# Gated mix of linear attention and FFN on one core: keys and values by seven block products, FFN weights streamed through the first sweep, the query fold moved to TensorE

## The chip, the cores and the metric

The kernel runs on one core of a Trainium2 chip. The core has TensorE (PE in the profile; its weight loads are shown apart as PEld), VectorE (DVE), ScalarE (ACT), GpSimd (POOL) and SyncE (SP, which here only issues DMAs). The metric is the device time of one execution in microseconds. The kernel before took 514.8 us, the median of three runs (514.75 to 515.55).

## The reference

The input is one sequence of 2048 rows with 512 features. A gate mixes two branches: linear attention with 32 heads of 16 features, and an FFN with 1792 hidden units.

```python
g = sigmoid((x * gate_w).sum(-1, keepdims=True))
out = g * A(x) + (1 - g) * B(x)

def A(x):                     # linear attention with a learned feature map
    q, k, v = heads(x @ wqkv)                          # 32 heads of 16
    pq, pk = q @ w_phi, k @ w_phi                      # one 16x16 matrix per head
    phi_q = concat([softmax(pq), softmax(-pq)])
    phi_k = concat([softmax(pk), softmax(-pk)])
    kv, z = phi_k.T @ v, phi_k.sum(over rows)          # per head
    return ((phi_q @ kv) / (phi_q @ z + 1e-6)) @ wo

def B(x):
    h = relu(x @ w1 + b1)
    return (h * h) @ w2 + b2
```

Keys must be summed over all 2048 rows before the first query row can be finished.

## The kernel before

**Arithmetic.** Every large product is computed in three matmuls: an operand is split into a high part, rounded by an ACT copy, and a low part, the difference, formed on DVE (`split`, one ACT and one DVE instruction). `mm3` then issues high x high, high x low and low x high into one PSUM bank. Each of these matmuls has 128 stationary columns and 512 moving columns.

**Loops.** The rows go in four blocks of 512 (`NB`), each of four chunks of 128 (`NC`). The FFN's hidden units go in 14 slices of 128. There are two sweeps over the four blocks: the first with hidden slices 0 to 6, the second with 7 to 13. A sweep, block and slice make one *work step* t, 56 in all. In work step t TensorE runs up(t+2), the first FFN product, 12 matmuls into a bank of `ps_u` (two banks), and down(t), the second product, 12 matmuls into the four banks of `ps_d`. Between them ACT and DVE make the hidden values of up(t) (`hidden`: ReLU, square, high part on ACT, then the low part `hl` on DVE). At the end of a block DVE evacuates the four `ps_d` banks (L714), and the first sweep's results go to DRAM as `part`. The FFN weights of a sweep's seven slices (`w1`, `w2`, high and low) are all held in SBUF, in a pool of seven.

**Slots.** Each work step has two slots, 2t before up(t+2) and 2t+1 before down(t). A table (`at(slot, function, ...)`) places all other work in these slots. The code is written in slot order, and a list scheduler turns it into one in-order queue for each engine, by priorities: `high_priority` raises one, and `issue_after` ties an instruction behind another.

**First sweep.** For each chunk, `do_k` projects the keys (12 matmuls, `k`) into the bank of `ps_a`; DVE reads them four times and ACT and DVE make the two softmaxes (`exps`, `scaled`). `do_v` projects the values (12 matmuls, `v`), which ACT copies to `vext`. For every two chunks `do_kv` adds phi_k.T @ [v, 1] into one bank, `kvps`, which stays in `ps_b` during the whole sweep. The gate's dot products, block loads and splits, and the saving of the split x to DRAM (`xkept`) lie between.

**The folds.** w_phi is multiplied into wk and wq once. For wk this is 64 small matmuls (`foldk`, in the place of up(3) at work step 1) into four PSUM banks, and four DVE transposes. For wq it is done on DVE: 64 DMAs that read rows of wq with repetition, and 64 multiply-adds (L234, L236) spread over slots 13 to 46, then transposes and a trip through DRAM.

**Second sweep.** For each chunk `do_q` projects the queries, `q_phi` makes features and denominators (POOL multiplies by z, L363), the features are transposed by DVE and DMAs, and `numer` and `attended` finish the attention.

Of the kernel before, what the change touches and what calls it, by code (L numbers as in the profile page):

```python
# [16 lines left out]
P = 128  # L17
# [7 lines left out]
LAG = 2  # L25
NG = 8
VW = DH + 1
NV = 3
AHEAD = 150


@with_exitstack
def tile_gated_mix(ctx: ExitStack, tc: tile.TileContext, xT, xn, wqT, wkT, wphi, wv, wo, w1, b1, w2, b2, gw, out):
# [6 lines left out]
    fpool = pool("fpool", NFH)  # L40
# [27 lines left out]
    def mm3(o, a, b, sa, sb, first, last):  # L68
        (ah, al), (bh, bl) = a, b
        nc.tensor.matmul(o, ah[:, sa], bh[:, sb], start=first, stop=False)  # L70
        nc.tensor.matmul(o, ah[:, sa], bl[:, sb], start=False, stop=False)  # L71
        return nc.tensor.matmul(o, al[:, sa], bh[:, sb], start=False, stop=last)  # L72
# [12 lines left out]

    def ffn_tiles(nm, fc):
        return (fpool.tile([P, 512], F32R, tag=nm + "h", name=f"{nm}h{fc}"),
                fpool.tile([P, 512], F32R, tag=nm + "l", name=f"{nm}l{fc}"))
# [13 lines left out]
    def ready(nm, fc):  # L102
        hi, lo = ffn_tiles(nm, fc)
        i = split(raw.pop((nm, fc)), hi, lo, nc.scalar, nc.vector)
        (up_w if nm == "w1" else down_w)[fc] = hi, lo
        return i

    def ready_later(nm, fc):
        with tc.issue_after(st["act"].ins):
            ready(nm, fc)  # L110
# [20 lines left out]
    def x_fetch(b):  # L131
        for k in range(NK):
            if k % 2 == 0:
                t = work.tile([P, 2 * D], F32, tag="tb", name="xin", bufs=2)
            raw["x", b, k] = t[:, (k % 2) * D:(k % 2 + 1) * D]
            nc.sync.dma_start(raw["x", b, k], xT[b, :, k, :])
# [20 lines left out]
    wqm = dram.tile([NK * 4, 32, D], F32, name="wqm")  # L157
    zrow = dram.tile([2 * D], F32, name="zrow")
    xkept = dram.tile([NB, NK, 2, P, SB], F32, name="xkept")
    vext = [hold.tile([P, H * VW], F32, tag="vz", name=f"vext{i}") for i in range(NV)]  # L160
# [7 lines left out]
    def load_fold(wT):  # L168
        t = [row() for _ in range(1 + NK)]
        nc.sync.dma_start(t[0], wphi)  # L170
        for g in range(NK):
            nc.sync.dma_start(t[g + 1], wT[:, g, :])
        return t

    def foldk():
        wph, *t = st["wT"]  # L180
        pss = [ps_u.tile([P, 512], F32, tag="u", name=f"foldk{r}") for r in range(2)]
        pss += [p.tile([P, 512], F32, tag="s", name="foldk") for p in banks]
# [14 lines left out]
        w = work.tile([P, 2, 4, NG, 32], F32, tag="phiT", name="wkin", bufs=1).rearrange(  # L197
# [5 lines left out]
        banks.pop()  # L203
        st["wk"] = [w[:, k].rearrange("p g r s -> p (g r s)") for k in range(NK)]

    def foldk_ready(k):
        hi = wpool.tile([P, 512], F32R, tag=f"wah{k}", name=f"wkh{k}")
        lo = wpool.tile([P, 512], F32R, tag=f"wal{k}", name=f"wkl{k}")
        with tc.high_priority(offset=AHEAD):
            split(st["wk"][k], hi, lo, nc.scalar, nc.vector)  # L210
        st.setdefault("wa", []).append((hi, lo))

    def foldq_numbers():
        wph = st["wT"][0]
        t = stage.tile([P, 512], F32, tag="in", name="wpht")
        st["phc"] = small.tile([P, NK, DH], F32, tag="dz", name="phc", bufs=2)  # L220
        with tc.issue_after(st["low"].ins):
            nc.vector.transpose(t, wph)

            nc.vector.tensor_reduce(st["phc"], t.rearrange("p (g j e) -> p g e j", g=NK, e=DH), AX.X, ALU.add)

    def foldq_step(i):
        g, e = divmod(i, DH)
        t = stage.tile([P, 512], F32, tag="in", name="wqr")
        nc.sync.dma_start(t, wqT.rearrange("(j e) g d -> g e j d", e=DH)[g, e].unsqueeze(1).to_broadcast([8, DH, D]))
        s = st["phc"][:, g, e:e + 1]  # L230
        with tc.issue_after(st["low"].ins):
            if e == 0:
                st["acc"] = row()
                nc.vector.tensor_scalar(st["acc"], t, s, None, ALU.mult)  # L234
            else:
                nc.vector.scalar_tensor_tensor(st["acc"], t, s, st["acc"], op0=ALU.mult, op1=ALU.add)  # L236
        if e == DH - 1:
            if g == 0:
                st["wqt"] = work.tile([P, 2, 4, NG, 32], F32, tag="phiT", name="wqt", bufs=1).rearrange(
                    "p u r g s -> p (u r g s)").rearrange("p (c g j) -> p c g j", c=4 * NK, g=NK)  # L240
            nc.vector.transpose(st["wqt"][:, :, g, :], st["acc"].rearrange("p (c j) -> p c j", c=4 * NK))

    def foldq_move():
        for r in range(4):
            nc.sync.dma_start(wqm.rearrange("c i (r n) -> r i c n", r=4)[r],
                              st["wqt"][32 * r:32 * r + 32].rearrange("p c g j -> p c (g j)"))
        st["wq"] = [row() for _ in range(NK)]
        for k in range(NK):
            nc.sync.dma_start(st["wq"][k], wqm[4 * k:4 * k + 4].rearrange("c i n -> (c i) n"))

    def foldq_ready(k):
        hi = wpool.tile([P, 512], F32R, tag=f"wah{k}", name=f"wqh{k}")
        lo = wpool.tile([P, 512], F32R, tag=f"wal{k}", name=f"wql{k}")
        v = lambda t: t.rearrange("p (g r j) -> p g r j", g=NK, r=4)
        with tc.high_priority(offset=AHEAD):
            split(st["wq"][k].rearrange("p (r g j) -> p g r j", g=NK, r=4), v(hi), v(lo), nc.scalar, nc.vector)
        st.setdefault("waq", []).append((hi, lo))
        if k == NK - 1:
            st["wa"] = st["waq"]
# [8 lines left out]
    def v_ready(k):  # L268
        hi, lo = w_tiles("v", k)
        with tc.issue_after(st["act"].ins):  # L270
            split(raw.pop(("v", k)), hi, lo, nc.scalar, nc.vector)
        st.setdefault("wb", []).append((hi, lo))

    def w_tiles(nm, k):
        return (wpool.tile([P, 512], F32R, tag=f"wbh{k}", name=f"w{nm}h{k}"),
                wpool.tile([P, 512], F32R, tag=f"wbl{k}", name=f"w{nm}l{k}"))

    def load_w(src, nm):
        res = []
        for k in range(NK):  # L280
            if nm == "o":

                t = stage.tile([P, 512], F32, tag="in", name="in")
                for q in range(4):
                    s = 64 * (4 * (k % 2) + q) + 32 * (k // 2)
                    nc.sync.dma_start(t[32 * q:32 * q + 32, :], src[s:s + 32, :])
            else:
                t = load(src[k * P:(k + 1) * P, :])
            hi, lo = w_tiles(nm, k)
# [5 lines left out]
    def gate_load(n):  # L295
        t = st["xn", n] = work.tile([P, D], F32, tag="ol" if n % 2 else "oh", name="xn", bufs=2)
        nc.sync.dma_start(t, xn[n])
# [52 lines left out]
    def kv_chunk(n, kvps, phi, v):  # L350
        for i in range(NG):
            for j in range(4):
# [3 lines left out]
                                 start=(n == 0 and i == 0), stop=(n == NB * NC - 1),  # L356
# [105 lines left out]
    def do_w(src, nm):  # L462
# [304 lines left out]
```

## Time and profile before

| what | value |
|---|---|
| median of three runs | 514.8 us |
| profiled execution: first to last instruction (span) | 513.7 us |
| around the span, median less span | 1.1 us |
| granted TensorE clock | 1.000 |
| PE, PEld, DVE, ACT, POOL busy | 509.4, 411.3, 401.0, 227.3, 44.1 us |
| POOL, first sweep | idle but for memsets |
| DMA moved | 75.4 MB, 147 GB/s over the span |

The profile is one execution. A row of its time line reads: start, duration, engine, source line, operation, output <- inputs, shapes, count, and in brackets the idle time before it with what ended it. A row of its groups reads: line, engine, operation, output <- inputs, shapes, count | busy time, mean ns of one | idle before. Matmuls overlap: each takes about 0.39 us from start to end, while the next begins before that, so their pace is read from the starts of their weight loads. DVE and ACT instructions overlap a little in the same way.

### The profile page before, as it was taken

What the parts mean: (1) busy time and instruction counts of PE and PEld (TensorE: products, weight loads), DVE (VectorE), ACT (ScalarE), POOL (GpSimd) and SP (SyncE); (2) the same over time, 40 slices, a digit from 0 to 9 for tenths busy, and PEclk for the clock granted to TensorE, in tenths of its full rate; (3) what the DMA queues carried; (4) which work ended last, traced back from release to release, by engine and by line L of the source; (5) the groups of instructions that cost most, each with busy time, mean ns of one, the idle gap of its engine ahead of it and who ended that gap; (6) DMA issues with size and microseconds to landing.
All of it is one profiled execution on the core that took longest, in us unless ns stands there. A gap on an engine that the chain in (4) does not pass through costs nothing.

```text
span 513.7 us, 9257 instructions
## 1 busy us (share of the span) xinstructions
PE 509.4 (99%) x3536; PEld 411.3 (80%) x3536; DVE 401.0 (78%) x680; ACT 227.3 (44%) x390; POOL 44.1 (9%) x44
## 2 busy tenths in 40 slices
PE   9999999999999999999999999999999999999997
PEld 4888888888888888888888878788787878788876
DVE  3779769796998798787889787988779677797724
ACT  6676253254224344253854544242625353343530
POOL 1000000000000000000003040301111111201100
PEclk9999999999999999999999999999999999999999
DMA  8897535467554476548359152213153321032102
GB/s 300 290 329 236 160 119 161 142 210 245 201 157 147 156 255 223 189 139 225 107 167 342 40 163 77 92 42 103 35 167 106 85 77 48 3 101 82 41 24 82
DMA packets 48277, 75.35 MB, mean 147 GB/s; under 512 B 7016, under 2 KB 15464, under 8 KB 48232
## 3 DMA queue, kind: packets, MB, share of 16 engines
q1 hardware_dynamic: 47912, 74.35, 45.7%
q8 instruction: 28, 0.46, 0.4%
q10 hardware_dynamic: 288, 0.39, 0.2%
q14 instruction: 17, 0.14, 0.1%
q0 software_dynamic: 32, 0.01, 0.0%
HBM read 50.60 MB, written 17.83 MB: 133 GB/s over the span
## 4 chain that ended last, share of the span: by engine, by line
PE 98%; ACT 1%; DVE 0%; issue 0%
PE d L70 10%; PE u L70 10%; PE d L72 10%; PE d L71 10%; PE u L71 10%; PE u L72 10%; PE v L70 3%; PE k L70 3%; PE k L72 3%; PE q L70 3%; PE att L70 3%; PE q L71 3%; PE k L71 3%; PE att L72 3%; PE att L71 3%; PE q L72 3%
## 5 line engine op out<-in xcount | busy, mean ns | idle before, releaser
L435 ACT ACTIVATE r<-u,b1c 128x512 f32<-128x512 f32 x56 | 38.6, 689 | 163.0 <-PE u L72 162.6
L70 PE MATMUL d<-w2h,hh 128*128 128x512 f32 x222 | 86.7, 391 | 0.0
L72 PE MATMUL d<-w2h,hl 128*128 128x512 f32 x222 | 86.5, 389 | 0.0
L71 PE MATMUL d<-w2l,hh 128*128 128x512 f32 x222 | 86.4, 389 | 0.0
L70 PE MATMUL u<-xh,w1h 128*128 128x512 f32 x216 | 84.8, 393 | 0.0
L71 PE MATMUL u<-xl,w1h 128*128 128x512 f32 x216 | 84.1, 389 | 0.0
L72 PE MATMUL u<-xh,w1l 128*128 128x512 f32 x216 | 84.0, 389 | 0.0
L65 DVE TENSOR_TENSOR hl<-r,hh 128x512 fp32r<-128x512 f32 x56 | 37.8, 675 | 34.5 <-ACT hh L62 34.5
L339 DVE TENSOR_REDUCE sm<-e 128x64 f32<-128x1024 f32 x32 | 38.9, 1215 | 27.8 <-ACT e L336 27.8
L363 POOL TENSOR_TENSOR ez<-e,z 128x512 f32<-128x512 f32 x32 | 41.9, 1330 | 216.9 <-ACT e L336 210.8
L236 DVE SCALAR_TENSOR_TENSOR row<-wqr,phc,row 128x512 f32<-128x512 f32 x60 | 44.5, 742 | 6.6 <-DMA wqr<-in_wqT 6.2
L70 PEld LDWEIGHTS u<-xh,w1h 128*128 128x128 f32 x216 | 40.5, 188 | 11.1 <-issue 2.1
L70 PEld LDWEIGHTS d<-w2h,hh 128*128 128x128 f32 x222 | 41.7, 188 | 9.2 <-issue 0.6
L72 PEld LDWEIGHTS d<-w2h,hl 128*128 128x128 f32 x222 | 41.7, 188 | 8.7
L71 PEld LDWEIGHTS d<-w2l,hh 128*128 128x128 f32 x222 | 41.7, 188 | 8.6
L72 PEld LDWEIGHTS u<-xh,w1l 128*128 128x128 f32 x216 | 40.6, 188 | 8.5
L71 PEld LDWEIGHTS u<-xl,w1h 128*128 128x128 f32 x216 | 40.5, 188 | 8.2
L336 ACT ACTIVATE e<-e 128x1024 f32<-128x1024 f32 x32 | 33.8, 1057 | 24.0 <-DVE e L334 23.8
L387 ACT ACTIVATE phiT<-tb 32x256 f32<-32x256 f32 x64 | 26.5, 414 | 32.5 <-DVE tb L381 31.8
L62 ACT ACTIVATE hh<-r 128x512 fp32r<-128x512 f32 x56 | 35.3, 630 | 1.5
L436 ACT ACTIVATE r<-r 128x512 f32<-128x512 f32 x56 | 35.2, 628 | 1.1
L365 DVE TENSOR_REDUCE dz<-ez 128x64 f32<-128x1024 f32 x16 | 19.3, 1207 | 9.5 <-POOL ez L363 9.4
(116 smaller groups left out, 875.1 us busy)
## 6 DMA issues: line engine op xcount, KB each, us to landing
wqr<-in_wqT SPq DMA_DIRECT2D x64, 256.0 KB
in<-in_w SPq DMA_DIRECT2D x24, 256.0 KB
phiT<-tb SPq DMA_DIRECT2D x192, 32.0 KB
xin<-in_xT SPq DMA_DIRECT2D x16, 256.0 KB
xn<-in_xn SPq DMA_DIRECT2D x16, 256.0 KB
xkept<-xh SPq DMA_DIRECT2D x16, 256.0 KB
xkept<-xl SPq DMA_DIRECT2D x16, 256.0 KB
part<-row SPq DMA_DIRECT2D x16, 256.0 KB
```

The costliest lines, as they stand in the source:

```text
L62: i = nc.scalar.activation(hi, src, AF.Copy)
L65: st["low"] = elo.tensor_tensor(lo, src, hi.bitcast(F32), ALU.subtract)
L70: nc.tensor.matmul(o, ah[:, sa], bh[:, sb], start=first, stop=False)
L71: nc.tensor.matmul(o, ah[:, sa], bl[:, sb], start=False, stop=False)
L72: return nc.tensor.matmul(o, al[:, sa], bh[:, sb], start=False, stop=last)
L236: nc.vector.scalar_tensor_tensor(st["acc"], t, s, st["acc"], op0=ALU.mult, op1=ALU.add)
L336: nc.scalar.activation(ef, ef, AF.Exp)
L339: nc.vector.tensor_reduce(sm, e3, AX.X, ALU.add)
L363: nc.gpsimd.tensor_tensor(ez[:, hs, :], e3[:, hs, :], zbc[half], ALU.mult)
L387: nc.scalar.activation(dst, src, AF.Copy)
L435: nc.scalar.activation(r, ps, AF.Relu, bias=b1c[:, fc:fc + 1])
L436: nc.scalar.activation(r, r, AF.Square)
```

## The change

**Seven products.** The first sweep takes two chunks together (a *pair* p of 0 to 7). Let A be their 256 rows x 512 features, cut into four blocks (A12 is the first chunk with the second half of the features), and B the 512 x 1024 matrix [wk, wv] cut into B11, B21 (wk) and B12, B22 (wv). The four results (keys and values of each chunk) come from seven products of a 128-row block with a 256 x 512 block, by sums of the rows (S1 to S4) and of the weights (T1 to T4). A product is six matmuls. POOL forms the sums (`sums_make` once, `rows_make` per pair), ACT and DVE split them (`operand_ready`, `rows_ready`). The seven products `p1` to `p7` use three PSUM tiles: X and Z in `ps_a` (`kx`, `kz`), Y in `ps_b` (`ky`). Between products intermediate results are read out: ACT copies A11 x B11 to `t1`; DVE adds `t1`, `t2` or `t15` to a PSUM tile while that tile is still accumulated into. The second chunk's features are made from an SBUF tile, `k2`.

**The kv sum.** `ps_b` is no longer free, so a pair's phi_k.T @ [v, 1] goes to a `ps_u` bank and DVE adds it to an SBUF tile `kvs` (four instructions per pair).

**Streamed FFN weights.** The pool of weight tiles has three slots, not seven (`NSTR`). From work step 7 on every w1 and w2 slice is loaded and split again for each block: 42 more loads through the four `stage` buffers, 42 more ACT copies, and the low parts on POOL (`ready_later(..., nc.gpsimd)`). The second sweep's weights are split from slot 48 on rather than 44. The gate's rows of x now go through `stage` too.

**The query fold.** wq is folded like wk: 64 small matmuls (`fold("q")`) at slot 7 into the two `ps_u` banks, `ps_a` and `ps_b`, four transposes, and a trip through DRAM.

The core of the diff:

```diff
-NV = 3
+NV = 2
+NSTR = 3
-    fpool = pool("fpool", NFH)
+    fpool = pool("fpool", NSTR)
...
+    def sums_make(kk, early):
+        k1, k2, v1, v2 = st["w", "k"][kk], st["w", "k"][2 + kk], raw["v", kk], raw["v", 2 + kk]
+        t1, t4 = [raw.setdefault((op, kk), row()) for op in ("T1", "T4")] if early else (raw["T1", kk], raw["T4", kk])
+        raw["T2", kk], raw["T3", kk] = v2, v1
+        for o, x, y in ((t1, v1, k1), (v1, v2, v1)) if early else ((v2, v2, t1), (t4, k2, v2)):
+            nc.gpsimd.tensor_tensor(o, x, y, ALU.subtract)
...
+        for i, x, y, op in ((0, part_of(a, 1), part_of(c, 1), ALU.add), (1, o[0], part_of(a, 0), ALU.subtract),
+                            (2, part_of(a, 0), part_of(a, 1), ALU.subtract), (3, part_of(c, 0), o[1], ALU.subtract)):
+            nc.gpsimd.tensor_tensor(o[i], x, y, op)
...
+    def p1(p):
+        st["X", p] = ps_a.tile([P, 512], F32, tag="s", name="kx")
+        product(st["X", p], p, "A11", "B11", True, False)
+        st["t1", p] = kept("t1")
+        with tc.high_priority(offset=AHEAD):
+            nc.scalar.activation(st["t1", p], st["X", p], AF.Copy)
+
+    def p6(p):
+        st["Y", p] = ps_b.tile([P, 512], F32, tag="s", name="ky")
+        product(st["Y", p], p, "S2", "T2", True, False)
+        st["t2", p] = kept("t2")
+        total(st["t2", p], st["Y", p], st["t1", p])
+
+    def p2(p):
+        product(st["X", p], p, "A12", "B21", False, True)
+        features(2 * p, st["X", p])
...
+    def p4(p):
+        product(st["Y", p], p, "A22", "T4", False, True)
+        t = kept("k2")
+        total(t, st["Y", p], st["t1", p])
+        features(2 * p + 1, t)
...
+    for t in range(NFH, NB * NFH):
+        for nm, s in (("w1", 2 * t - 5), ("w2", 2 * t - 2)):
+            at(s - 3, fetch, nm, t % NFH)
+            at(s, ready_later, nm, t % NFH, nc.gpsimd)
+
+    for kk in range(2):
+        for op, s in (("B11", 3), ("B22", 4), ("B21", 5), ("T2", 6), ("T1", 8), ("T3", 9), ("T4", 10)):
+            at(s, operand_ready, op, kk)
+    for kk in range(2):
+        at(3, sums_make, kk, True)
+        at(4, sums_make, kk, False)
...
+    for p in range(NPAIR):
+        s = 8.5 + 5.5 * p
+        for f, d in ((p1, 0), (p6, 1), (p2, 1), (p5, 3), (p7, 3), (p4, 4), (p3, 4)):
+            at(s + d, f, p)
+        at(min(s + 7.5, NB * SL - 3), do_kv, p)
...
-    for i in range(NK * DH):
-        at(13 + i * 0.51, foldq_step, i)
+    at(3, foldq_load)
+    at(7, fold, "q")
```

Three queues change at places that the prediction speaks of.

ScalarE, around work steps 3 to 5. Before, between the hidden values of up(4) and the ReLU (L435) of up(5), it makes the high parts of one w1 and one w2 slice, of wv, and one exponential (L336):

```order
L62 ACTIVATE hh<-r 128x512
L62 ACTIVATE w1h_446<-in 128x512
L62 ACTIVATE w2h_450<-in 128x512
L62 ACTIVATE wvh_454<-wvin 128x512
L62 ACTIVATE wvh_458<-wvin 128x512
L62 ACTIVATE wvh_502<-wvin 128x512
L62 ACTIVATE wvh_506<-wvin 128x512
L336 ACTIVATE e<-e 128x1024
L435 ACTIVATE r<-u,b1c 128x512
```

In the changed kernel the same stretch holds the copies of B21 and of T2, whose source `wvin` POOL rewrites in place:

```order
L65 ACTIVATE hh<-r 128x512
L65 ACTIVATE w1h_472<-in 128x512
L65 ACTIVATE w2h_476<-in 128x512
L65 ACTIVATE B210h<-wkin 128x512
L65 ACTIVATE B211h<-wkin 128x512
L65 ACTIVATE T20h<-wvin 128x512
L65 ACTIVATE T21h<-wvin 128x512
L435 ACTIVATE r<-u,b1c 128x512
L436 ACTIVATE r<-r 128x512
L65 ACTIVATE hh<-r 128x512
L65 ACTIVATE w1h_538<-in 128x512
```

The ReLU of up(5) now stands behind a copy that waits for POOL.

GpSimd, after its memsets. Before, its next work is the multiplication by z in the second sweep:

```order
L155 MEMSET kvb 128x256
L163 MEMSET vext_111 128x32
L163 MEMSET vext_112 128x32
L163 MEMSET vext_113 128x32
L553 MEMSET row 128x256
L363 TENSOR_TENSOR ez<-e,z_3069 128x512
```

In the changed kernel (L237 makes the weight sums T, L256 the row sums S of pairs 0, 1 and 2, L68 the low parts of streamed weights):

```order
L237 TENSOR_TENSOR row<-wvin,wkin 128x512 x2
L237 TENSOR_TENSOR wvin<-wvin 128x512 x2
L256 TENSOR_TENSOR row<-xin 128x256 x2
L256 TENSOR_TENSOR row<-row,xin 128x256
L256 TENSOR_TENSOR row<-xin,row 128x256
L237 TENSOR_TENSOR wvin<-wvin,row 128x512
L237 TENSOR_TENSOR row<-wkin,wvin 128x512
L237 TENSOR_TENSOR wvin<-wvin,row 128x512
L237 TENSOR_TENSOR row<-wkin,wvin 128x512
```

The row sums of pair 1 stand ahead of both T2 sums, the `wvin<-wvin,row` rows, of which the second feeds the copy T21h.

TensorE, from the end of up(5) into down(3). Before, the value projection of chunk 0 follows up(5), then down(3), then the keys of the next chunk:

```order
L72 MATMUL u<-xh_3_176,w1l_447 128x512
L70 MATMUL v<-wvh_454,xh_0_161 128x512
L71 MATMUL v<-wvl_455,xh_0_161 128x512
L72 MATMUL v<-wvh_454,xl_0_162 128x512
L70 MATMUL v<-wvh_458,xh_1_166 128x512
L71 MATMUL v<-wvl_459,xh_1_166 128x512
```

In the changed kernel:

```order
L75 MATMUL u<-xh_3_176,w1l_473 128x512
L74 MATMUL d_258<-w2l_477,hh 128x512
L75 MATMUL d_258<-w2h_476,hl 128x512
L73 MATMUL d_259<-w2h_476,hh 128x512
L74 MATMUL d_259<-w2l_477,hh 128x512
L191 MATMUL foldq_557<-fold 32x128
L191 MATMUL foldq<-fold 32x128 x2
```

No projection stands between up(4), down(2), up(5) and down(3) any more; the fold of wq (of which one matmul, into foldq_556, stands inside up(5)) comes inside down(3), and its second bank, foldq_557, is the one that up(5) used.

More of the change, by code (lines that the diff above doesn't have):

```diff
@@ L27 @@
 VW = DH + 1
-NV = 3
+NV = 2
+NPAIR = S // P // 2
+NSTR = 3
 AHEAD = 150
+SUMS = ("t1", "t2", "t15", "k2")
 @with_exitstack
@@ L217, in foldq_numbers @@
[L217 to L241, printed above, removed]
@@ L295, in gate_load @@
     def gate_load(n):
-        t = st["xn", n] = work.tile([P, D], F32, tag="ol" if n % 2 else "oh", name="xn", bufs=2)
-        nc.sync.dma_start(t, xn[n])
+        st["xn", n] = load(xn[n])
     def gate_dot(n):
```

248 lines of the change are left out of this document (138 added, 110 removed).

## Prediction

> **What bounds the kernel now.** I read the page's busy shares and the chain of waits first, then the list of who waited for whom, then the time line of TensorE's weight loads.
>
> ```profile
> span 513.7 us, 9257 instructions
> ...
> PE 509.4 (99%) x3536; PEld 411.3 (80%) x3536; DVE 401.0 (78%) x680; ACT 227.3 (44%) x390; POOL 44.1 (9%) x44
> ...
> PE 98%; ACT 1%; DVE 0%; issue 0%
> ```
> ```profile
> PEld kvps L354 <- issue: 2.8, 8, 0.4
> PEld k L70 <- ACT vext L531: 0.7, 2, 0.5
> ```
>
> The chain that ends last is TensorE for 98% of the span, and the waits of weight loads for another engine are tenths of a microsecond. So TensorE's own work is the span: a matmul removed is gained in full, and any wait of TensorE that the change brings is lost in full. DVE at 78% is the second engine; POOL has almost nothing to do.
>
> ```profile
> 17.31 0.19 PEld L72 LDWEIGHTS d<-w2h,hl 128*128 128x128 f32 x1
> 17.85 1.63 PEld L186 LDWEIGHTS foldk<-row 32*32 32x32 f32 x128 [0.35 <-ACT hh L62]
> 19.68 0.19 PEld L70 LDWEIGHTS d<-w2h,hh 128*128 128x128 f32 x1 [0.20 <-issue]
> ...
> 22.31 0.19 PEld L70 LDWEIGHTS u<-xh,w1h 128*128 128x128 f32 x1
> ...
> 25.03 0.19 PEld L70 LDWEIGHTS u<-xh,w1h 128*128 128x128 f32 x1
> ```
>
> up(3) starts at 22.31, up(4) at 25.03: 12 matmuls in 2.72 us, 0.227 us each.
>
> **Removed and added on TensorE.** Keys and values of two chunks took 4 x 12 = 48 matmuls and take 7 x 6 = 42: 6 fewer in each of 8 pairs, 48 x 0.227 = **-10.9 us**. The fold of wq has the 64 matmuls of foldk: from 17.31 to 19.68 less one matmul, **+2.1 us**. The kv matmuls keep their number. With no new wait this would be -8.8 us.
>
> **The other engines' totals.**
>
> ```profile
> L236 DVE SCALAR_TENSOR_TENSOR row<-wqr,phc,row 128x512 f32<-128x512 f32 x60 | 44.5, 742 | 6.6 <-DMA wqr<-in_wqT 6.2
> L583 DVE TENSOR_TENSOR row<-att,row 128x512 f32<-128x512 f32 x16 | 10.8, 677 | 5.0 <-PE att L72 5.0
> L557 DVE COPY row<-kvps 17x256 f32<-17x256 f32 x4 | 1.7, 421 | 1.2 <-PE kvps L354 1.2
> L65 DVE TENSOR_TENSOR hl<-r,hh 128x512 fp32r<-128x512 f32 x56 | 37.8, 675 | 34.5 <-ACT hh L62 34.5
> L336 ACT ACTIVATE e<-e 128x1024 f32<-128x1024 f32 x32 | 33.8, 1057 | 24.0 <-DVE e L334 23.8
> L703 ACT ACTIVATE row<-b2b,rest 128x512 f32<-128x512 f32 x16 | 10.8, 713 | 4.5 <-DVE rest L312 4.5
> ```
>
> DVE loses 44.5 us of multiply-adds. It gains 40 additions of a PSUM and an SBUF tile (like L583, 27.1 us), 32 kv additions (nearest the copy L557, 13.5) and 22 low parts (14.9): about 11 us more in a sweep of some 245. That alone is no bound. But nobody waited for the multiply-adds, while TensorE waits for the additions before it may write the same bank again. ACT gains some 60 copies, at 44% busy. POOL gets 42 low parts, 8 weight sums and 32 half-size row sums. DMA: 64 loads of wq rows go and 42 weight loads come, each 256 KB; the queue SP is in order, and its x load for block 1 now waits for POOL's S1 (the sums read the same buffer). I cost DMA at nothing: the splits that use these loads come 7 us or more after SP can issue them. If that cover is gone, the splits of up(6) and up(7) are late by as much.
>
> **What POOL work costs.** The trace has POOL beside DVE in the second sweep only.
>
> ```profile
> L363 POOL TENSOR_TENSOR ez<-e,z x32: 1275/1297/1854, 268.5 to 476.5; 128x512 f32<-128x512 f32 x32
> ```
> ```profile
> 268.51 3.11 POOL L363 TENSOR_TENSOR ez<-e,z 128x512 f32<-128x512 f32 x2 [49.51 <-ACT e L336]
> 277.67 2.55 POOL L363 TENSOR_TENSOR ez<-e,z 128x512 f32<-128x512 f32 x2 [6.04 <-DVE dz L365]
> ```
> ```profile
> 269.79 0.68 DVE L65 TENSOR_TENSOR w2l<-in,w2h 128x512 fp32r<-128x512 f32 x1
> ...
> 279.43 0.84 DVE L370 SCALAR_TENSOR_TENSOR den<-dz,eps 128x32 f32<-128x32 f32 x1
> ```
> ```profile
> L370 DVE SCALAR_TENSOR_TENSOR den<-dz,eps 128x32 f32<-128x32 f32 x16 | 4.6, 287 | 0.5
> ```
>
> A POOL instruction of 512 columns takes 1.27 us. A pair takes 2.55 us; where a DVE low part starts as the first ends (268.51 + 1.28 = 269.79), the pair takes 3.11, 0.56 more, the DVE instruction's length. The other way round, L370, with mean 0.29, takes 0.84 and ends at 280.27, just after POOL's pair (280.22). All these DVE instructions read two SBUF tiles. So I take POOL's instructions and DVE's with two SBUF inputs (all low parts, the gate's products, the scaling of features) as one after the other. The Trainium skill says the same of this pair (SBUF — State Buffer, "Who interferes with whom"): a DVE instruction with two SBUF inputs and a GpSimd one that reads SBUF exclude each other for a whole instruction, and the later one stands still. By that rule the sum is the one below; by the bare durations it is that of the first rival.
>
> **The start, term by term.** Until 18.4 us ACT's and DVE's queues are those of before.
>
> ```profile
> 19.33 0.69 DVE L65 TENSOR_TENSOR w2l<-in,w2h 128x512 fp32r<-128x512 f32 x1
> 19.93 2.50 DVE L201 STREAM_TRANSPOSE wkin<-foldk 128x512 f32<-128x512 f32 x4
> 23.13 2.50 DVE L65 TENSOR_TENSOR wkl<-wkin,wkh 128x512 fp32r<-128x512 f32 x4 [0.70 <-ACT wkh L62]
> ```
> ```profile
> 28.17 0.69 ACT L435 ACTIVATE r<-u,b1c 128x512 f32<-128x512 f32 x1 [0.70 <-PE u L72]
> 28.89 0.63 ACT L436 ACTIVATE r<-r 128x512 f32<-128x512 f32 x1
> 29.56 0.63 ACT L62 ACTIVATE hh<-r 128x512 fp32r<-128x512 f32 x1
> 30.10 0.62 ACT L62 ACTIVATE w1h<-in 128x512 fp32r<-128x512 f32 x1
> 30.62 0.61 ACT L62 ACTIVATE w2h<-in 128x512 fp32r<-128x512 f32 x1
> ```
>
> DVE's pace is 0.60 us per instruction (four in 2.50), ACT's 0.52 for a copy and 0.7 for ReLU and square. Two low parts of S (pair 0) now stand ahead of foldk's transposes, which end at 23.6 rather than 22.4; TensorE needs only the first by 22.3 and does not wait. At 23.6 POOL can begin T1. Up to T21 it has seven sums of 512 columns (8.9 us) and the four half-size S1, taken as half, 2.6. In the same stretch DVE has ten low parts (6.0). One after the other: 23.6 + 17.5 = 41.1, so T21 is done near 41.2 (without exclusion 35.2). The copy T21h then holds ACT to 41.8, and the ReLU of up(5) behind it ends at 42.5.
>
> TensorE: down(2) ends at 30.5, up(5) gets its high weights at 31.0 and its low ones, DVE taking turns with POOL, at 34.9; it comes to foldq_557 at 38.1 and waits for that ReLU until 42.5. The fold's rest (1.8) and seven matmuls of down(3) bring it to 45.9. up(6) needs foldq_556 transposed; ahead of that DVE has hl, two weights, two x tiles and T11, whose ACT copies follow the ReLU in a row and end at 46.4: the transpose ends at 48.1. Without a wait up(6) would start at 30.5 + 2.7 + 2.1 + 2.7 = 38.0. **+10.1 us** (without exclusion, by the same steps, 42.1: +4.1). The half-size sums could take a full 1.27 each: +2.5 more, an end of the range. Queued behind the waiting matmul are all of down(3) and up(6); behind T21h on ACT the ReLU, hidden values and two weight copies.
>
> **Pair 1.** From up(8)'s end to up(9) TensorE has 18 matmuls, 4.1 us. ACT has, ahead of up(8)'s ReLU, the exponential of pair 0's second chunk, which waits for DVE: k2's addition and four reads (3.0 us) come behind two low parts and two gate products that meet POOL, and end, by the same count, 1.2 us after up(8). Then exponential, ReLU, square, the b2 row, high part and weight copy: 0.95 + 0.72 + 0.66 + 0.65 + 0.54 + 0.62 = 4.1. The weights are ready after 5.4 us, 1.4 late; POOL's low part is 1.3 after that and wanted after two matmuls (0.45): 0.9 late. With 0.3 at a block's evacuation **+2.6** (without exclusion 0.7).
>
> **The other pairs.** Most streamed weights have 24 matmuls or more (5.4 us) between one up and the next, against 2.7 for ReLU to copy and 1.3 on POOL: hidden. Two more places have 18; I give them 0.4 each, and 0.2 for p1, which may write `ps_a` only after DVE has added the value tile (3.7 us of DVE against 4.1 to 5.4 on TensorE): **+1.0**. The kv bank in `ps_u` and the later second-sweep splits (two work steps of margin) I cost at nothing; if this cover fails, at most a DVE instruction each, 0.7.
>
> Sum: -10.9 + 2.1 + 10.1 + 2.6 + 1.0 = **+4.9 us**. The profiled span is 513.7, the median 1.1 above; 514.8 + 4.9 = **519.7 us**.
>
> **The rivals.**
> 1. POOL and DVE don't hold each other up. Against it stand the two rows above. Then -10.9 + 2.1 + 4.1 + 0.7 = -4.0: 510.8, faster. It decides where T21 ends: each microsecond earlier than 41.2 is one less of wait, and at 36.2 the sum is zero.
> 2. TensorE never waits: -8.8, 506.0. The ACT queue speaks against it.
> 3. DVE does not catch up, and the six later pairs lose 2.6 each: 519.7 + 15.6 - 1.0 = 534.3. For it: DVE's load; against it: no gate products with late loads and no operand splits after pair 1.
> 4. TensorE runs at half pace after its long wait. At the start it does:
>
> ```profile
> 9.16 0.19 PEld L449 LDWEIGHTS u<-xh,w1h 128*128 128x128 f32 x1 [0.24 <-ACT w1h L508]
> 9.59 0.19 PEld L449 LDWEIGHTS u<-xl,w1h 128*128 128x128 f32 x1 [0.24 <-issue]
> 9.82 0.19 PEld L449 LDWEIGHTS u<-xh,w1h 128*128 128x128 f32 x1
> ```
> ```profile
> 0.78 5.28 PE L476 MATMUL warm<-const-bfloat16-1.0 128*128 128x512 bf16 x12 [0.78 <-PEq L756]
> ```
>
> From 0.78 to 9.59 a matmul starts every 0.43 us, then every 0.23. Once more, 8.8 x (1 - 0.227 / 0.43) = 4.2 us, of which the wait for the transpose (2.2) hides half: 521.7. No later row shows it, but no later wait is that long. The Trainium skill (TensorE: Matmul & The Clock Gate, Part 1) has the clock halve after some 3.4 us of idling and recover after as much work; that would be an estimate of 1.7 us.
>
> **Chances.** Forecast 0.50; rival 1 0.20; rival 2 0.06; rival 3 0.08; rival 4 0.10; 0.06 that the waits come out near 8.8 us and nothing can be told (0.2%, 1.0 us, is about what a measurement of this kernel resolves). Faster 0.26, same 0.06, slower 0.68. The range 510.0 to 527.0 takes in rivals 1 and 4, S1 at full price and half of rival 3, and leaves out rival 2 and the rest of 3. The forecast's own range is 516.5 to 523.5.
>
> **What would show it.** In the changed profile: about 48 fewer large matmuls; TensorE's longest waits near 38 us at foldq, released by the ReLU, and before up(6), released by DVE's transpose; L237's last sum ending near 41; DVE low parts longer than 0.69 beside POOL; up(9) waiting for ACT and POOL; few waits after 100 us. I am wrong if T21 ends by 36 us, or if waits go on through all pairs.

## The result and the profile after

The changed kernel takes 534.5 us, the median of four runs (532.9 to 536.2), against 514.8 us: a ratio of 1.0375 (95% interval 1.0351 to 1.0399). It is slower, as forecast, but by 19.7 us where the prediction had 4.9, and outside its range of 510 to 527. A profile shows one execution and not the median; the one below took 532.9 us.

The page of the changed kernel, its span, its busy shares and its chain of waits:

```profile
span 531.1 us, 9626 instructions
...
PE 508.8 (96%) x3616; PEld 405.3 (76%) x3616; DVE 444.4 (84%) x704; ACT 256.6 (48%) x446; POOL 149.6 (28%) x125
...
PE 62%; issue 13%; DVE 11%; POOL 6%; DMA 5%; ACT 1%; SPq 1%; POOLq 0%; DVEq 0%; ACTq 0%
```

TensorE was 98% of the chain before and is 62% now. DVE lost the 44.5 us of multiply-adds and is nevertheless 43 us busier. The list of who waited for whom names the places (total in us, times, longest):

```profile
PEld ky L73 <- DVE vext L538: 5.6, 3, 2.6
PEld kx L73 <- DVE vext L538: 5.4, 3, 2.2
PEld foldq L191 <- ACT r L435: 3.8, 1, 3.8
...
PEld u L75 <- DVE w1l L68: 2.0, 1, 2.0
PEld u L73 <- ACT w1h L65: 1.8, 2, 1.3
...
PEld u L75 <- POOL w1l L68: 1.5, 2, 1.1
PEld d L73 <- DVE row L768: 1.2, 1, 1.2
```

The two largest are waits that the prediction priced at almost nothing: a product may not write its PSUM bank (`kx` by product 1, `ky` by product 4) before DVE has added the bank to the value tile (L538). To put numbers on stages I counted, from the starts of TensorE's weight loads, all time beyond 0.24 us per start wherever two starts lie more than 0.25 us apart. This holds waits and stretches of half clock alike.

| waits of TensorE, us | before | changed | more |
|---|---|---|---|
| the start, 16 to 52 us | 0.9 | 8.9 | 8.0 |
| pair 1 and the end of block 0, 60 to 91 us | 0.6 | 5.1 | 4.5 |
| the rest of the first sweep | 2.3 | 16.6 | 14.3 |
| second sweep | 4.6 | 4.6 | 0.0 |

With 10.9 us of matmuls removed and 2.1 for the fold this gives +18.0; the spans differ by 17.4. Gaps beside the fold are counted twice here, in its 2.1 and in the start. The second sweep, unchanged in its work, is unchanged in time.

**The start** went by the predicted chain. These are the second T2 sum on POOL, the copy of it and the ReLU behind it on ScalarE, and the fold on TensorE:

```profile
37.55 1.71 POOL L237 TENSOR_TENSOR wvin<-wvin,row 128x512 f32<-128x512 f32 x1
```
```profile
39.29 0.63 ACT L65 ACTIVATE T21h<-wvin 128x512 fp32r<-128x512 f32 x1 [2.72 <-POOL wvin L237]
39.83 0.67 ACT L435 ACTIVATE r<-u,b1c 128x512 f32<-128x512 f32 x1
```
```profile
33.66 0.19 PEld L75 LDWEIGHTS u<-xh,w1l 128*128 128x128 f32 x1 [1.96 <-DVE w1l L68]
...
40.55 2.35 PEld L191 LDWEIGHTS foldq<-fold 32*32 32x32 f32 x126 [3.84 <-ACT r L435]
```

T21 is done at 39.3 us (forecast: 41.2, and 35.2 without exclusion), and the fold waits 3.84 us for the ReLU. Its matmuls then take 2.35 us rather than the 1.63 that foldk took. The granted clock in stretches of 3.4 us (columns: stretch, length, busy time of PE, PEld, DVE, ACT and POOL, granted clock, DMA share, GB/s) says why:

```profile
36.20:39.60 3.40, 0.93 (x5) 0.43 (x3) 3.40 (x3) 0.68 (x2) 3.32 (x3) 1.00 0.92 294
39.60:43.00 3.40, 2.45 (x126) 2.12 (x126) 2.88 (x4) 3.34 (x7) 1.33 (x1) 0.50 1.01 373
43.00:46.40 3.40, 3.40 (x28) 2.26 (x8) 3.40 (x7) 2.98 (x6) 0.73 (x1) 0.50 0.64 140
46.40:49.80 3.40, 3.40 (x16) 2.60 (x16) 3.40 (x6) 0.04 (x1) 1.92 (x3) 1.00 1.00 378
73.70:77.10 3.40, 1.91 (x8) 1.07 (x7) 3.40 (x7) 2.30 (x6) 2.23 (x2) 1.00 0.19 73
77.10:80.50 3.40, 3.40 (x10) 2.62 (x9) 3.28 (x8) 0.39 (x1) 0.74 (x1) 0.51 0.75 208
```

After the wait TensorE runs at half clock for 6.8 us, and once more for 3.4 us at pair 1, from 77.1 us, after two waits of 1.3 and 1.1 us. The first of these stretches hides a wait. up(6) begins at 46.43 us, and the bank that it writes was free only when the first of DVE's four transposes was done, near 46.1:

```profile
45.47 2.50 DVE L206 STREAM_TRANSPOSE wqin<-foldq 128x512 f32<-128x512 f32 x4
```

**The later pairs.** DVE's queue ahead of product 4 of a pair at the end of block 1:

```profile
144.69 0.69 DVE L303 SCALAR_TENSOR_TENSOR in<-in,gwb 128x512 f32<-128x512 f32 x1 [2.60 <-DMA in<-in_xn]
...
148.17 2.73 DVE L768 SCALAR_TENSOR_TENSOR row<-d,rest,row 128x512 f32<-128x512 f32 x4
150.82 0.68 DVE L538 TENSOR_TENSOR t<-kz,t 128x512 f32<-128x512 f32 x1
...
151.88 0.62 DVE L538 TENSOR_TENSOR vext<-ky,t 128x512 f32<-128x512 f32 x1
```
```profile
152.55 0.19 PEld L73 LDWEIGHTS ky<-T40h,xh 128*128 128x128 f32 x1 [2.60 <-DVE vext L538]
```

A gate row arrives late, DVE stands for 2.6 us, and everything behind it in its queue is late, the additions last. The row's load (`in`) was issued only at 140.84 us, behind a load of the next block's x (`xin`), and that one waited for POOL's row sums, which read the buffer that it overwrites:

```profile
139.66 0.74 POOL L256 TENSOR_TENSOR row<-xin 128x256 f32<-128x256 f32 x1
```
```profile
140.42 0.33 SPq L145 DMA_DIRECT2D xin<-in_xT  x1
140.84 0.38 SPq L83 DMA_DIRECT2D in<-in_xn  x1
```

For the only other late gate row DVE stands for 3.4 us, up to 209.97. Its load was issued at 207.17, when POOL had ended a low part (207.14) and released one of the four `stage` buffers that gate rows share with the streamed weights. So POOL's work also holds up loads. And many of DVE's instructions are simply longer than before, by groups:

```profile
L68 DVE TENSOR_TENSOR hl<-r,hh 128x512 fp32r<-128x512 f32 x29 | 30.6, 1053 | 3.1 <-ACT hh L65 3.1
...
L334 DVE TENSOR_TENSOR e<-mn,k 128x512 f32<-128x512 f32 x8 | 8.7, 1090 | 0.0
...
L334 DVE TENSOR_TENSOR e<-mn,kx 128x512 f32<-128x512 f32 x8 | 5.4, 674 | 0.0
```

These are the first sweep's. The low part `hl` has a mean of 1,053 ns where it had 675 over the kernel before. The last two rows are the same instruction on the same shapes: 1,090 ns where the keys lie in SBUF (`k`), 674 ns where they lie in PSUM (`kx`). Of these two, only the form with two SBUF inputs is stretched.

### The profile page after: what moved, and what is told of

Same layout as the page of the kernel before. It is cut to its first block, busy times and chain, and to the rows that moved or that the text cites. A ratio compares the mean times of both kernels' runs of the same rounds, so it can differ in the third digit from the quotient of the medians.

```text
span 531.1 us, 9626 instructions
## 1 busy us (share of the span) xinstructions
PE 508.8 (96%) x3616; PEld 405.3 (76%) x3616; DVE 444.4 (84%) x704; ACT 256.6 (48%) x446; POOL 149.6 (28%) x125
## 4 chain that ended last, share of the span: by engine, by line
PE 62%; issue 13%; DVE 11%; POOL 6%; DMA 5%; ACT 1%; SPq 1%; POOLq 0%; DVEq 0%; ACTq 0%
PE d L73 6%; PE d L75 6%; PE d L74 6%; PE u L73 6%; PE u L74 6%; PE u L75 6%; PE q L73 3%; PE q L75 3%; PE att L75 3%; PE att L73 3%; PE q L74 3%; PE att L74 3%; POOL w2l L68 2%; POOL row L256 2%; DMA in<-in_w 2%
## 5 line engine op out<-in xcount | busy, mean ns | idle before, releaser
L435 ACT ACTIVATE r<-u,b1c 128x512 f32<-128x512 f32 x56 | 38.4, 685 | 122.7 <-PE u L75 122.3
L73 PE MATMUL d<-w2h,hh 128*128 128x512 f32 x160 | 63.7, 398 | 0.7 <-DVE row L768 0.7
L68 POOL TENSOR_TENSOR w1l<-in,w1h 128x512 fp32r<-128x512 f32 x21 | 28.5, 1356 | 124.9 <-ACT w1h L65 106.1
L75 PE MATMUL d<-w2h,hl 128*128 128x512 f32 x160 | 63.2, 395 | 0.0
L74 PE MATMUL d<-w2l,hh 128*128 128x512 f32 x160 | 63.0, 393 | 0.0
L75 PE MATMUL u<-xh,w1l 128*128 128x512 f32 x152 | 60.1, 395 | 2.3 <-DVE w1l L68 1.6
L73 PE MATMUL u<-xh,w1h 128*128 128x512 f32 x152 | 60.6, 399 | 1.0 <-ACT w1h L65 0.9
L74 PE MATMUL u<-xl,w1h 128*128 128x512 f32 x152 | 59.8, 393 | 0.0
L68 DVE TENSOR_TENSOR hl<-r,hh 128x512 fp32r<-128x512 f32 x56 | 48.5, 867 | 13.1 <-ACT hh L65 13.0
L336 ACT ACTIVATE e<-e 128x1024 f32<-128x1024 f32 x32 | 33.9, 1059 | 46.6 <-DVE e L334 46.3
L339 DVE TENSOR_REDUCE sm<-e 128x64 f32<-128x1024 f32 x32 | 38.9, 1216 | 20.3 <-ACT e L336 20.2
L387 ACT ACTIVATE phiT<-tb 32x256 f32<-32x256 f32 x64 | 26.5, 413 | 31.6 <-DVE tb L381 30.9
L75 PEld LDWEIGHTS u<-xh,w1l 128*128 128x128 f32 x152 | 28.8, 190 | 9.5 <-DVE w1l L68 2.0
L436 ACT ACTIVATE r<-r 128x512 f32<-128x512 f32 x56 | 35.2, 628 | 1.2
L73 PEld LDWEIGHTS u<-xh,w1h 128*128 128x128 f32 x152 | 28.7, 189 | 9.3 <-ACT w1h L65 1.8
L68 POOL TENSOR_TENSOR w2l<-in,w2h 128x512 fp32r<-128x512 f32 x21 | 33.1, 1575 | 8.7 <-issue 8.2
```

The source lines that it names most:

```text
L68: st["low"] = elo.tensor_tensor(lo, src, hi.bitcast(F32), ALU.subtract)
L336: nc.scalar.activation(ef, ef, AF.Exp)
L339: nc.vector.tensor_reduce(sm, e3, AX.X, ALU.add)
L387: nc.scalar.activation(dst, src, AF.Copy)
L435: nc.scalar.activation(r, ps, AF.Relu, bias=b1c[:, fc:fc + 1])
L436: nc.scalar.activation(r, r, AF.Square)
```

## The experiments

**One part at a time.** First, the kernel before with only the query fold moved to TensorE:

```diff
-    at(8, foldq_numbers)
-    for i in range(NK * DH):
-        at(13 + i * 0.51, foldq_step, i)
+    at(4, load_fold, "q", wqT)
+    at(9, foldq)
```

> The kernel before with only the query fold moved to TensorE (at slot 9, through four row buffers), neither seven products nor streamed weights. Theory: the fold costs its own TensorE time, 64 small matmuls or about 2.1 us, and no wait, and the 44.5 us that DVE loses gain nothing, since nobody waited for them: 516.9 us (516 to 518). Rival: the fold's four banks and its transposes make TensorE wait as at the start of the changed kernel, 519 us or more. Second rival: TensorE was held by DVE after all, 514.8 us or less.

Measured: 518.4 us, ratio 1.0058 (1.0043 to 1.0073), 3.2 us more than the kernel before: just above the theory's range, below the first rival. That is 2.1 for the fold and about 1 at the end of the first sweep, where the transposition of the sums comes to wait for something that the profile doesn't name:

```profile
PEld kvt L547 <- issue: 1.1, 1, 1.1
```

So the fold's own price fits, and DVE's 44.5 us gained nothing. Then the FFN weights streamed in addition:

```diff
+    for t in range(NFH, NB * NFH):
+        for nm, s in (("w1", 2 * t - 5), ("w2", 2 * t - 2)):
+            at(s - 3, fetch, nm, t % NFH)
+            at(s, ready_later, nm, t % NFH, nc.gpsimd)
```

> The same with the FFN weights streamed through three slots in the first sweep, low parts on POOL, but keys and values still as eight products. Theory: streaming adds waits of up to 2 us in all, since without the seven products nobody on TensorE waits for a DVE addition: 517 to 519 us. Rival: loads and splits of the streamed weights are late block after block and are what the changed kernel loses in its later pairs: 525 us or more.

Measured: 521.9 us, ratio 1.0127 (1.0112 to 1.0142), 3.5 us more, above the theory's range and well below the rival. The page and the waits:

```profile
PE 512.1 (98%) x3664; PEld 412.1 (79%) x3664; DVE 380.7 (73%) x614; ACT 248.9 (48%) x432; POOL 106.8 (21%) x86
```
```profile
PEld k L72 <- ACT vext L513: 1.7, 2, 1.5
...
PEld k L72 <- DVE wqin L203: 1.6, 1, 1.6
```

DVE executes the same 614 instructions as without streaming, where it was 361.4 us busy: 42 POOL low parts (63 us of POOL) add 19.3 us to DVE's busy time without giving it any work. TensorE loses little by it: of its long waits here only one, of 1.6 us, is for DVE. The seven products, with what comes with them (the kv sum, the gate rows in `stage`), then account for the other 12.6 us: 10.9 gained, some 23 lost in waits.

**Is it POOL's reading?** The changed kernel, with POOL's low parts replaced by one column and zeros:

```diff
-        st["low"] = elo.tensor_tensor(lo, src, hi.bitcast(F32), ALU.subtract)
+        s = slice(0, 1 if elo is nc.gpsimd else 512)
+        st["low"] = elo.tensor_tensor(lo[:, s], src[:, s], hi.bitcast(F32)[:, s], ALU.subtract)
+        if elo is nc.gpsimd:
+            with tc.issue_after(st["low"].ins):
+                st["low"] = elo.memset(lo.bitcast(F32)[:, 1:], 0.0)
```

> The changed kernel, but POOL makes only the first column of each low part of a streamed weight and fills the rest with zeros, so that 42 POOL instructions read almost nothing (this leaves out the low parts of the streamed weights; the order of the queues is nearly unchanged). Theory: DVE instructions stretched by POOL are why the DVE additions come late in the pairs after the first; most of these 13 us of waits go, and pair 1 loses its half clock too: about 523 us (519 to 527). Rival: the order of DVE's queue and its load make the additions late, POOL's reads hardly matter: 531 us or more.

Measured: 522.6 us, ratio 1.0133 (1.0113 to 1.0152), 11.9 us less. The theory holds.

```profile
PE 504.6 (97%) x3616; PEld 403.8 (78%) x3616; DVE 424.5 (81%) x704; ACT 255.8 (49%) x446; POOL 118.0 (23%) x167
```

DVE's same 704 instructions take 20 us less. By the count above, pair 1 waits 1.5 us rather than 5.1, the later pairs 9.9 rather than 16.6; the start has 9.7 beside 8.9. Of those 9.9 the two largest waits, with a stretch of half clock behind them, follow the first of two late gate rows. DVE still stood 6.2 us for gate rows; the load of that first one again stood behind an x load that waited for POOL's row sums, which this version keeps. The zeros also make POOL itself 31.6 us less busy, so they remove its reads and its own lateness together; TensorE's direct waits for POOL's low parts were only 1.5 us, though.

The start is the same here up to the fold, 3.8 us of wait included, but this execution has no half clock there, and now the wait for the transposes is seen. up(6) begins as late as in the changed kernel:

```profile
46.14 0.47 PE L75 MATMUL u<-xh,w1h 128*128 128x512 f32 x1 [2.08 <-DVE wqin L208]
```

What if DVE does these low parts itself?

```diff
-            at(s, ready_later, nm, t % NFH, nc.gpsimd)
+            at(s, ready_later, nm, t % NFH)
```

> The changed kernel with the 42 low parts of streamed weights on DVE and no longer on POOL. DVE gets 42 x 0.6 = 25 us of work and loses about 20 us of stretching (its busy time went from 444.4 to 424.5 us where POOL read nothing). Theory, that the two engines exclude each other, so that a POOL instruction costs DVE as much as one of its own: within 4 us of the changed kernel, 531 to 536 us. Rival, that POOL only slows DVE a little and that the engine is well chosen: 540 us or more, since DVE is the late engine and gets a tenth more work.

Measured: 522.2 us, ratio 1.0141 (1.0125 to 1.0157): better than both expectations, by as much as leaving the work out.

```profile
PE 509.5 (98%) x3616; PEld 403.5 (78%) x3616; DVE 447.8 (86%) x746; ACT 256.8 (49%) x446; POOL 88.0 (17%) x83
```

42 more instructions, some 25 us of work, make DVE 3.4 us busier: the stretching cost nearly as much as the work. By the count, pair 1 waits 1.3 us and the later pairs 8.9. Why TensorE waits so much less is only partly shown. No gate row is late any more: DVE never stands for one. No wait of products 1 and 4 for an addition is longer than 0.4 us. But the scheduler, which now expects these low parts later, also cut TensorE's order into smaller pieces (2 matmuls of one product, 10 of the next), and many waits became small ones of 0.3 to 0.5 us. How the 12 us divide among these causes wasn't told apart.

The third way is to do the low parts once. Each streamed weight is split in block 0, its two parts go to DRAM and come back by two loads per block:

```diff
+    def w_reload(nm, fc):
+        t = ffn_tiles(nm, fc)
+        for j in range(2):
+            nc.sync.dma_start(t[j].bitcast(F32), wkept[nm == "w2", fc, j])
...
-            at(s, ready_later, nm, t % NFH, nc.gpsimd)
+            at(s, w_reload, nm, t % NFH)
```

> The changed kernel, but each streamed weight is split once, in the first block; its two parts go to DRAM and come back by two loads in the later blocks, so 42 ACT copies and 42 POOL low parts go, and 28 stores and 42 more loads of 256 KB come. All results stay whole. Theory: with POOL's reads of the low parts gone, DVE is late less often, as with the zeros (522.6): 523 us (520 to 526). Rival: the further 18 MB of transfers, in order on one queue, come late and take what POOL's rest gives back: 530 us or more.

Measured: 517.6 us, ratio 1.0048 (1.0033 to 1.0063), better than expected: the later pairs' waits fall to 4.7 us. The loads of raw weights no longer share buffers with the gate rows, and 42 copies on ScalarE go as well. Here too DVE never stands for a gate row.

**The start.** First by the table alone:

```diff
-(1, 3, 12)
+(1, 5, 12)
-("T2", 6), ("T1", 8)
+("T2", 7), ("T1", 8)
```

> The changed kernel with two numbers of its table changed: the row sums of pair 1 are made in slot 5 rather than 3, so that POOL makes the T2 sums before them, and T2 is split in slot 7 rather than 6, so that its copies stand behind the ReLU of up(5). Theory: the wait of 3.8 us at the fold goes, and with it the stretch of half clock behind it (2.1 us): 534.5 - 5.9 = 528.6 us (527 to 530). Rival: the next copy or sum in line takes the place of the wait, and less than 2 us is gained: 532.5 us or more.

Measured: 533.9 us, ratio 1.0361 (1.0342 to 1.0379). The rival holds. The wait at the fold is gone, and these stand in its place:

```profile
PEld u L75 <- DVE w1l L68: 2.5, 1, 2.5
...
PEld u L73 <- ACT xh L65: 1.8, 1, 1.8
```

The start's count is 8.6 us beside 8.9, with its half clock 6 us earlier, and up(6) begins hardly earlier, once more held by the transposes:

```profile
45.80 0.47 PE L73 MATMUL u<-xh,w1h 128*128 128x512 f32 x1 [1.42 <-DVE wqin L206]
```

So T21 was a link of a chain, not its cause: in all three executions up(6) begins when DVE, stretched by POOL, has come to the transposes. With the eight weight sums on DVE:

```diff
-            nc.gpsimd.tensor_tensor(o, x, y, ALU.subtract)
+            nc.vector.tensor_tensor(o, x, y, ALU.subtract)
```

> The changed kernel with the eight sums of weights (T1 to T4) on DVE and no longer on POOL. Theory: in the start ten DVE low parts and these sums then take 0.6 us each instead of 1.1 to 1.7 beside POOL, so T21 is done near 34 us rather than 39.3, the wait at the fold (3.8 us) and its half clock go, and up(5)'s low weights (2.0 us) come in time: 534.5 - 6 = 528.5 us (526 to 531). Rival: DVE has no room in the start, and the sums push its low parts and transposes back by as much: 533 us or more.

Measured: 530.5 us, ratio 1.0291 (1.0274 to 1.0309), 4 us less, at the slow end of the theory: the start's count falls from 8.9 to 4.7, in a profiled execution of 527.5 us that has no half clock. up(6) begins at 42.0 us. What stays is the wait of up(6) that the prediction had as its second:

```profile
PEld u L73 <- DVE wqin L206: 2.8, 1, 2.8
```

**DVE's order.** Product 3 before product 4, in the changed kernel:

```diff
-(p7, 3), (p4, 4), (p3, 4)
+(p7, 3), (p3, 4), (p4, 4)
```

> The changed kernel with one pair of entries of its table swapped: product 3 stands before product 4 in each pair, so DVE adds the value tile of the first chunk, which frees the bank that the next pair's product 1 writes, before it adds and reads the second chunk's keys five times. Theory: the waits of product 1 (5.4 us in three places, released by that addition) go, those of product 4 (5.6 us) stay: 534.5 - 5 = 529.5 us (528 to 532). Rival: DVE's load is all that counts, and product 4 or the next one waits for what is now later: 533 us or more.

Measured: 533.8 us, ratio 1.0343 (1.0316 to 1.0371). The rival fits better, though the four runs scatter from 531.4 to 535.4. The waits for the value tile went, and product 3, now the earlier one, waits for another addition of the same queue:

```profile
PEld kz L73 <- DVE t L538: 5.7, 3, 2.8
PEld u L75 <- POOL w1l L68: 4.9, 7, 1.1
```

As long as DVE is behind, whichever product comes next waits.

**Together.** The reloaded weights, the weight sums on DVE and the two changes of the table at the start:

> The changed kernel with the reloaded weights, the sums of weights on DVE, the row sums of pair 1 in slot 5 and T2's split in slot 7, all together. Theory: the gains of reload (11 us) and of the sums (6 us) lie in different stages and add up: 534.5 - 17 = 517 us (513 to 521), near the kernel before. Rival: the waits move on to the next late copy or addition, as they did where the table alone was changed: 524 us or more.

Measured: 515.3 us, ratio 1.0013 (0.9994 to 1.0032): the gains add up, and it is level with the kernel before. The waits that are left:

```profile
PEld u L73 <- ACT w1h L65: 3.0, 2, 2.0
PEld u L73 <- ACT T10h L65: 2.9, 1, 2.9
...
PEld kx L73 <- DVE vext L549: 2.2, 3, 1.7
```

All low parts and weight sums on DVE, without reloading, with the fold in slot 6 and product 3 first:

> The changed kernel with the weight sums and the 42 low parts on DVE, the row sums of pair 1 in slot 5, T2's split in slot 7, product 3 before product 4, and the fold of wq in slot 6, before up(5): POOL keeps only the row sums. Theory: the gain of the low parts (12 us) and those of the start (6 to 8 us) add up: 515 us (512 to 518). Rival: DVE, with some 30 us more work than in the version that reloads, becomes late again: 520 us or more.

Measured: 519.8 us, ratio 1.0093 (1.0072 to 1.0113), between the two expectations: in the profiled execution (522.2 us) the start's count is only 3.2 us, the later pairs' still 9.8.

The version at 515.3 with product 3 first and the fold of wq in slot 6:

```diff
-    at(7, fold, "q")
+    at(6, fold, "q")
```

> The version with reloaded weights and sums on DVE (515.3 us), with product 3 before product 4 and the fold of wq in slot 6, before up(5), where DVE stood idle for 3 us. Theory: the wait of up(6) for the transposes (2.9 us), that of up(5) for its high weights (1.0 us) and those of product 1 (2.3 us) go, so 515.3 - 5.5 = 509.8 us (508 to 512), faster than the kernel before. Rival: ScalarE's copies in the start take the transposes' place, and no more than 2 us is gained: 513 us or more.

Measured: 513.4 us, ratio 0.997 (0.9956 to 0.9985). With DVE no longer behind, the exchange of products 3 and 4 does what it should: no product waits for an addition. But the fold now stands still. Of these waits 1.1 us are for its loads, which are queued behind stores; for the longest, 3.6 us, the profile names no cause:

```profile
PEld foldq L202 <- issue: 4.0, 2, 3.6
...
PEld foldq L202 <- DMA fold<-in_wqT: 1.1, 2, 0.8
```

> The same, but the first slice of w1 isn't saved: it is loaded and split again in block 1 and saved then, so that w1's fourth slice needn't wait for the store out of the slot that it takes (2.0 us of TensorE in the version at 515.3). Theory: 2 us less than the version beside it. Rival: the stores of the next slices, one behind the other on the same queue, hold it up as long: the same within 0.7 us.

Measured: 513.3 us, ratio 0.9962 (0.9947 to 0.9977): no gain, as the rival had it, but for another reason. The wait for the copy is gone, and the fold's waits have grown instead. Here the first w1 slice is split again in block 1:

```diff
+            if nm == "w1" and t == NFH:
+                at(s - 3, fetch, nm, t % NFH)
+                at(s + 1, ready_later, nm, t % NFH)
```

Last, with the loads of wq ahead of the stores:

```diff
-    at(3, foldq_load)
+    at(1, foldq_load)
```

> The version at 513.25 us with the four loads of wq issued in slot 1, ahead of the stores of split weights on the same queue, rather than in slot 3 behind them. Theory: the fold's waits (about 5 us) and the half clock behind them (2.5 us) go, and nothing else waits: 513.25 - 6.5 = 506.8 us (505.5 to 509), the sum of the removed and added matmuls alone. Rival: the loads of block 1's x or ScalarE's copies are next in line and take half of it: 510 us or more.

Measured: 510.8 us, ratio 0.9917 (0.9902 to 0.9931): the fastest of all, 4.6 us below the kernel before, but short of 506.8. The fold's waits are down to 0.4 us, and the one without a named cause is gone too. The rival was right that others were next in line:

```profile
PE 503.3 (99%) x3616; PEld 404.5 (79%) x3616; DVE 420.1 (82%) x713; ACT 234.5 (46%) x405; POOL 73.6 (14%) x75
```
```profile
PEld u L73 <- DVE wqin L217: 1.5, 1, 1.5
...
PEld u L73 <- ACT w1h L65: 1.3, 1, 1.3
...
PEld d L74 <- DVE w2l L68: 0.8, 1, 0.8
```

The count is 5.7 us in the start, some 1.5 of them half clock after these waits, and 3.0 in the later pairs, 0.8 more than in the kernel before. With POOL's row sums on DVE as well:

> The same with the 32 half-size row sums on DVE too, so that POOL does nothing in the first sweep. Theory: POOL's 33 us of row sums stretch DVE by about as much as the sums cost on DVE (32 x 0.36 = 11.5 us), and TensorE waits for neither: the same within 1 us. Rival: without any POOL reads DVE is earlier and another 1 to 2 us is gained.

Measured: 512.6 us, ratio 0.9951 (0.9938 to 0.9964), 1.8 us slower, which neither side expected. The profiled executions differ by 0.7 us only, 0.2 of it in the start; the rest stays open.

## Why the prediction was wrong, step by step

- **-10.9 and +2.1**, the matmuls: right. The fold alone costs 2.1 us and about 1 us of waits elsewhere.
- **+10.1, the start**: right in mechanism and nearly in size. It waits 8.0 us more and its fold ran 0.7 us longer, 8.7 in all. The first wait was forecast from 38.1 to 42.5 us and was 36.7 to 40.6; T21 came at 39.3, between the count with exclusion and the one without, and nearer the first: the two engines took turns, but each turn was some 0.2 us shorter than the sum (1.70 us rather than 1.87). The second wait, for the transposes, was forecast to end at 48.1; up(6) began at 46.4. The list of waits doesn't have it, because half clock kept TensorE busy until then. In the zeros' run, without half clock, up(6) waited 2.5 us and began at 46.1.
- **+2.6, pair 1**: the two late operands were as forecast (1.4 and 0.9 us; measured 1.29 and 1.05). The 3.4 us at half clock behind them, 1.6 lost, and an evacuation late by 1.1 rather than 0.3 were missing.
- **+1.0, the other pairs**: this step failed. Measured: 14.3. The prediction gave product 1's wait 0.2, counting 3.7 us of unstretched DVE work against 4.1 to 5.4 on TensorE, and gave product 4's none; they are 5.4 and 5.6 us, and two more waits, 1.1 at a product 4 and 1.8 at the last kv product, end as DVE comes to the work that they need. Waits that "go on through all pairs" were the prediction's own sign of being wrong. Exclusion was used for the start and for pair 1 and then dropped, though the low parts that POOL makes go on through the whole sweep. The zeros show that with their reads gone 6.7 of the 14.3 go. The second cause lies in DMA, which was put at nothing. The prediction named the x load that waits for POOL's sums, but gave its cover for the splits of x alone, not for the gate row behind it in the queue. Two gate rows come late and DVE stands 6 us for them; how much of the rest that is wasn't measured by itself.
- **Rival 3**, the backlog in all later pairs, had the right place and nearly the size (15.6 us), with a chance of 0.08. That its total of 534.3 comes within 0.2 us is luck: it took pair 1's 2.6 six times over, and the measured terms differ from its own in every stage. The reason against it was mostly false: gate products come in every block, two of them late, and x splits and row sums' low parts take the place of the operand splits.
- **Rival 4**, half pace: it was priced after one long wait, and the reason against it was that no later wait is that long. It happened twice, the second time after waits of 1.3 and 1.1 us. The two slowed TensorE by some 2.1 and 1.6 us, but the first only stood in place of the wait for the transposes. The rival had half of it hidden there; nearly all of it was.
- **DVE's totals**: "about 11 us more in a sweep" counted the instructions at their undisturbed length. POOL's reads added some 20 us to that.

## What to carry to other kernels

When work moves to an idle engine, price what its reads do to the neighbour's instructions for as long as it runs, not only where two queues visibly meet: 63 us of low parts on the idle POOL cost the busy DVE 20 us, almost what doing them itself would. What the idle engine reads also stays occupied until it is done: look for loads that wait for these buffers, and for what stands behind them in the queue. When a change lets a bound engine wait for an engine that nobody waited for, recount that engine's whole queue, stage by stage, with every late load in it; moving single entries of the order only moves the wait. What has been computed once and is needed again can be cheaper to reload than to recompute on any engine.

## What the runs showed of the hardware that was not expected

**Which DVE instructions POOL stretches.** Besides the two forms of L334 above: the sums of exponentials, which read one SBUF tile, kept their length (1,214 ns before, 1,216 after), and so did the additions of a PSUM and an SBUF tile (about 680 ns beside 677 for L583). Those with two SBUF inputs went from 0.68 to between 1.2 and 1.8 us beside POOL in the start. The Trainium skill (SBUF — State Buffer, "Who interferes with whom") names just this pair of port users, and the traces agree on who is hit. In the start both queues were full: beside POOL's sums of 512 columns (1.27 us alone) DVE's low parts started every 1.70 us, beside those of 256 (0.74 alone) every 1.14. Whole turns with DVE's 0.60 us would give 1.87 and 1.34, so the two took turns, with some 0.2 us of overlap in each.

**Half clock comes in fixed stretches, after partial idling.** In the fifteen profiles of the changed kernel and the experiments, leaving out the ends, there are 15 stretches of half clock. Each begins a whole number of 3.413 us after the first full-clock moment of its profile, and each lasts 3.413 or 6.827 us. In the 3.413 us ahead of each TensorE stood idle for 2.07 to 3.09 us, by the starts of its weight loads. No stretch followed a window with less than 2.07; three windows with 2.15, 2.21 and 2.24 weren't followed by one, so the count isn't the exact rule. The Trainium skill (TensorE: Matmul & The Clock Gate, Part 1) has a free-running window of this length, which agrees, and the halving after at least one idle window; here 2.07 us of a window sufficed. A kernel with such waits scatters: in the version at 515.3, the five runs with granted clock 1.000 took 514.0 to 514.8 us, the three with 0.997 took 515.9 to 516.8, the two with 0.993 took 517.8 to 518.3. The changed kernel's four runs span 3.3 us, the kernel before's 0.8, but its times don't follow the granted clock, so there half clock isn't shown to be the reason.
